# Third batch's routing and the first expert's tokens in a hash-attention and mixture-of-experts kernel: one-hot, low keys and first gathers earlier in GpSimd's row, both turns ahead of their reading, and ScalarE rounding two pieces of w2

## The chip, the cores and the metric

The kernel runs on one core of one Trainium2 chip. A core has TensorE (PE in the rows; PEld is its weight load), VectorE (DVE), ScalarE (ACT), GpSimd (POOL) and the queue of SyncE (SP) from which most transfers are issued. The metric is the time of one execution in microseconds (us), lower is better. Unprofiled executions are given as a median; a profiled one gives the rows.

## The reference

```
# attention: q, k, v of (batch 4, heads 8, seq 768, dim 64), proj (64, 6)
q_bucket, k_bucket = hash of the signs of q @ proj and k @ proj      # 6 bits
scores = where(q_bucket == k_bucket, q @ k.T / 8, -1e9)
x = (softmax(scores) @ v), heads side by side -> (3072 tokens, 512)
# experts: 8, each 512 -> 1024 -> 512
logits = x @ w_gate;  e = argmax(logits);  gate = max of softmax(logits)
eom = sigmoid(x @ w_output_gate)[e]
out[token] = gate * eom * (relu(x[token] @ w1[e]) @ w2[e])
```

Everything is float32. A product that needs float32 precision is made of three matmuls of rounded operands: each operand is split in a rounded high part and a low part (value minus high part), and high x high, high x low and low x high are added.

## The kernel before

**Attention.** 32 heads are taken as 16 pairs (8 heads per batch, so four pairs per batch), 12 steps per pair, 192 steps in all. A step is one block of 128 queries of one head against 768 keys: `scores` (8 matmuls, L609, into a buffer of `ps_s`), a minimum on VectorE (L612), `soft` (exponential on ScalarE, L620), `normal` (row sums on VectorE, L627 and L628, then one multiplication per step on GpSimd, L630), `transposed` (12 transposes, L659, and copies to `pts` by ScalarE and VectorE, L666), and, per six steps, `weighted` (24 matmuls with v, L677). `transposed` runs six steps behind `scores`. The next pair's keys and queries are split into high and low parts ahead of their use: the low keys `kl` of a head are written by GpSimd (`split_lo`, L561) and read by the third term of `scores`.

**Order.** The order on each engine is written by hand: an instruction stands in its engine's row where the program issues it, and each engine works its row in order. The main loop goes through the steps two at a time. `plan(step, f)` puts a piece of other work at the end of a step; `block(step, when, f)` puts it into a step that is a multiple of six, where the order is: scores, two exponentials, "early", normals, "amid", two exponentials, normals, "before", "matmuls" (the 24 of `weighted`), "behind", then an exponential and `transposed` of two steps.

**Routing.** When a batch's attention is done, its tokens are routed during the next batch's steps: `best` (row maximum and exponentials), `equal`, `lowest`, `one_hot`, `prefix` (matmuls that count tokens per expert), `offsets`, `own_ranks`, chunk places, columns of a table (`column2`, `column0`, `column1` on GpSimd, `hot0` to `hot2` on VectorE), `table` (6 matmuls, L266) and `entries` (VectorE adds them, L270 and L271). `ROUTE` holds the steps for this; its second row is for the third batch, whose routing begins at step 144 (18 stands for step 162).

**First expert ahead.** After the third batch the expert with the most tokens so far is picked, and 256 of its tokens start early. `early_load` (SyncE) brings w1 in four pieces, `early_w1` splits each in two halves on GpSimd (high part L1008, low part L1009, 512 of 1024 columns each), `early_gather` makes the token numbers from the table (`lead_slots` on VectorE) and issues two indirect gathers of 128 rows each on GpSimd (L295), and `early_turn` transposes them on TensorE (L309) and rounds and splits them on VectorE (L311, L312). `late` is step 168, so `late + 24` is step 192, the first one without `scores`.

**Tail.** After step 197 come, interleaved: the first expert's upward products (`fill(0)` to `fill(7)`, 12 matmuls each, L355; ScalarE's relu, L365; the low part on VectorE, `low()`, L366), `weighted` of the last block, four pieces of w2 (`w2_piece`: load, high part, low part), and the last batch's routing on VectorE, up to its table. `w2_piece(..., "h")` makes the high part on GpSimd (L180) and the low part on VectorE (L183); "hl" makes both on GpSimd, "l" the low part on GpSimd and the high part on ScalarE (L182), which no piece of the first expert has in the kernel before. Pieces 4 and 6 are loaded into the space of a `pts` buffer, pieces 0 and 2 into the two `w_raw` buffers that held w1's third and fourth pieces. After this the downward products and the other experts follow.

Of the kernel before, what the change touches and what calls it, by code (L numbers as in the profile page):

```python
# [54 lines left out]
def f32(ap):  # L55
    return ap.bitcast(F32)
# [3 lines left out]
def lsh_attention_then_moe(  # L60
# [241 lines left out]
    def turn(xgn, xs, c0, px=None):  # L302

        xg, n = xgn
        early = px is not None
        if not early:
            px = ps_t.tile([P, NCC, CH], F32, name="ps_t")
        for cc in range(NCC):
            nc.tensor.transpose(px[:, cc, 0:n], xg[0:n].rearrange("n (p b) -> n b p", b=NCC)[:, cc], ident[0:n, 0:n])  # L309
        xh, xlo = (x[:, :, c0:c0 + n] for x in xs)  # L310
        (nc.vector.tensor_copy if early else nc.scalar.copy)(xh, px[:, :, 0:n])  # L311
        nc.vector.tensor_tensor(xlo, px[:, :, 0:n], f32(xh), ALU.subtract)  # L312
# [120 lines left out]
    with ExitStack() as actx:  # L433
# [19 lines left out]
                 ((18, "best"), (20, "equal"), (22, "lowest"), (22, "one_hot"), (24, "own_ranks"), (26, "chunk_hot"),  # L453
                  (28, "chunk_pos"), (28, "gate_sums"), (30, "hot0"), (31, "column2"), (32, "gate_values"),
                  (33, "column0"), (34, "hot1"), (36, "gate_parts"), (37, "gate_product"), (37, "column1"),
# [441 lines left out]
        for b in range(B - 1):  # L897
            r = routing(b)
            s0 = 12 * (H // 2) * (b + 1)
            for hf in range(2):  # L900
                block(s0 + PER * (hf + 1), "before", lambda r=r, hf=hf: r["logits"](hf, H // 2))
            for n, when, name in ((12, "before", "tokens0"), (18, "before", "tokens1"),
                                  (30 if b < B - 2 else 24, "before", "prefix"),
                                  (30 if b < B - 2 else 24, "before", "offsets"),
                                  (48 if b < B - 2 else 42, "before", "table"),
                                  (48 if b < B - 2 else 42, "before", "entries")):
                block(s0 + n, when, r[name])
            for n, name in ROUTE[b == B - 2]:
                plan(s0 + n, r[name])
# [83 lines left out]
        def early_turn(a):  # L993
            if a == 0:
                early["x"] = new_x0()
                early["px"] = ps_s.tile([P, 2, 512], F32, name="ps_s")
            turn(early["xg"][a], early["x"], a * CH, early["px"][:, a].rearrange("p (b n) -> p b n", b=NCC))

        def early_load(cc):
            early.setdefault("raw", []).append(w1_load(0, cc))  # L1000

        def early_w1(cc, h):
            if h == 0:
                early.setdefault("w1", []).append(
                    [wpool.tile([P, F], F32R, name="w1" + n, bufs=NCC) for n in "hl"])
# [7 lines left out]
        plan(late + 18, early_gather)  # L1013
        for a in range(EARLY):
            block(late + 24, ("early", "amid")[a], lambda a=a: early_turn(a))
        for cc in range(NCC):
            plan(late + (4, 5, 11, 15)[cc], lambda cc=cc: early_load(cc))
            for h in range(2):
                if (cc, h) == (NCC - 1, 1):
                    block(late + 24, "behind", lambda cc=cc, h=h: early_w1(cc, h))  # L1020
                else:
                    plan(late + (8, 10, 13, 14, 16, 19, 20)[2 * cc + h], lambda cc=cc, h=h: early_w1(cc, h))

        with tc.manual_schedule(engines=MANUAL | {mybir.EngineType.SP}):
# [98 lines left out]
            for f in (0, 4, 6, 2):  # L1123
                raw = spare[:, (f - 4) * DM:(f - 2) * DM].rearrange("p (f d) -> p f d", f=2) if f >= 4 else None
                pieces[f] = w2_piece(ep, 0, f, "h" if f in (0, 4) else "hl", raw)
# [11 lines left out]
            fill(2)  # L1137
            r["best"]()
            low()
# [240 lines left out]
```

## Time and profile before

| | us |
|---|---|
| median of 3 runs (lowest, highest) | 705.07 (704.32, 706.34) |
| the profiled execution's own time | 706.62 |
| its span, first to last instruction | 704.8 |
| granted TensorE clock, mean over the span | 0.993 |

The span is what the rows cover; times in rows count from its start. A timeline row gives start, duration, engine, line, operation, output and inputs, the number of merged instructions, and in brackets how long the engine had been idle and what ended that. The granted clock is a share of 2.4 GHz: 1.00 is the full clock, 0.50 is 1.2 GHz.

### The profile page before, as it was taken

The page shows a single profiled execution, that of the slowest core. Times are in us where ns is not written, and L with a number is a line of the kernel's source. Part 1 is how long each engine was busy: PE and PEld are TensorE (multiplying, and loading weights), DVE is VectorE, ACT ScalarE, POOL GpSimd, SP SyncE. Part 2 cuts the span into 40 slices and gives each one's busy share as a digit, 9 for nine tenths or more (in the row PEclk, how much of TensorE's full clock was granted, in tenths as well). Part 3 has the DMA queues.
Part 4 walks back from the last instruction along what each step waited for, and adds up shares of the span by engine and source line. Part 5 has one row for each costly group of instructions (what it writes and reads, how often), then busy time and mean ns, then how long its engine had stood idle before and what let it go on. Part 6 is the DMA issues. An engine that isn't in the chain of part 4 may idle for free. (4 is left out here: it accounts for less than half of the span.)

```text
span 704.8 us, 17360 instructions
## 1 busy us (share of the span) xinstructions
PE 686.8 (97%) x6591; PEld 540.6 (77%) x6591; DVE 460.1 (65%) x1012; ACT 437.9 (62%) x894; POOL 422.5 (60%) x550
## 2 busy tenths in 40 slices
PE   8999999999999999998997999999999999999996
PEld 5667676666767676766664789889999999989895
DVE  7888887888887888876865744453536454556340
ACT  5888998889898988887975124433426253434231
POOL 6767866577765778565898646354372727374201
PEclk9999999999999999999999999999999999999999
DMA  5554544354544545433335235533455544545401
GB/s 173 148 130 105 125 120 104 86 121 119 118 106 87 128 109 120 119 69 78 109 84 138 59 95 194 204 113 118 166 166 168 158 159 161 170 142 191 155 6 43
DMA packets 85283, 87.47 MB, mean 124 GB/s; under 512 B 57167, under 2 KB 67591, under 8 KB 85192
## 3 DMA queue, kind: packets, MB, share of 16 engines
q1 hardware_dynamic: 79704, 72.88, 38.6%
q0 software_dynamic: 5200, 13.31, 5.9%
q8 instruction: 54, 0.88, 0.5%
q14 instruction: 37, 0.30, 0.1%
q10 hardware_dynamic: 288, 0.10, 0.1%
HBM read 59.57 MB, written 13.11 MB: 103 GB/s over the span
## 5 line engine op out<-in xcount | busy, mean ns | idle before, releaser
L630 POOL TENSOR_SCALAR sc<-sc,rsum 128x768 f32<-128x768 f32 x192 | 172.2, 915 | 82.1 <-ACT pts L666 41.6
L612 DVE TENSOR_SCALAR_CACHE_REDUCE sc<-ps_s 128x768 f32<-128x768 f32 x192 | 176.3, 955 | 22.6 <-PE ps_s L609 20.7
L620 ACT ACTIVATE sc<-sc,mn 128x768 f32<-128x768 f32 x192 | 178.8, 950 | 3.8 <-DVE sc L612 3.7
L609 PE MATMUL ps_s<-kh,qhl 64*128 64x384 f32 x768 | 148.2, 400 | 1.4 <-DVE sc L612 0.8
L677 PE MATMUL ps_a<-pts,vt 128*64 128x384 f32 x768 | 134.3, 500 | 0.0
L666 ACT COPY pts<-ps_t 128x384 f32<-128x384 f32 x188 | 92.8, 494 | 36.3 <-PE ps_s L659 28.7
L677 PEld LDWEIGHTS ps_a<-pts,vt 128*64 128x64 f32 x768 | 53.5, 139 | 68.6 <-issue 61.5
L366 DVE SCALAR_TENSOR_TENSOR hl<-ps_s,hh 128x256 fp32r<-128x256 f32 (+8 forms) x40 | 34.0, 849 | 108.2 <-ACT hh L365 108.2
L377 POOL DMA_INDIRECT out_dram<-yo,sid x29 | 30.8, 1063 | 112.7 <-ACT yo L372 52.0
L355 PE MATMUL ps_s<-xh,w1h 128*128 128x256 f32 (+7 forms) x288 | 96.9, 337 | 0.6 <-DVE eq L748 0.6
L659 PEld LDWEIGHTS ps_t<-ident,sc 64*128 64x128 f32 x1140 | 81.9, 139 | 20.1 <-POOL sc L630 10.2
L329 POOL DMA_INDIRECT xq<-x_dram,idx x75 | 82.6, 1101 | 23.8 <-issue 19.9
L355 PE MATMUL ps_s<-xlo,w1h 128*128 128x256 f32 (+7 forms) x288 | 95.4, 331 | 0.0
L355 PE MATMUL ps_s<-xh,w1l 128*128 128x256 f32 (+7 forms) x288 | 95.4, 331 | 0.0
L365 ACT ACTIVATE hh<-ps_s 128x256 fp32r<-128x256 f32 (+8 forms) x40 | 29.1, 727 | 96.6 <-PE ps_s L355 95.3
L659 PE MATMUL ps_t<-ident,sc 64*128 64x64 f32 x1140 | 86.5, 223 | 0.0
L609 PEld LDWEIGHTS ps_s<-kh,qhl 64*128 64x128 f32 x768 | 76.1, 187 | 4.3 <-DVE sc L612 2.2
L609 PE MATMUL ps_s<-kl,qhl 64*128 64x384 f32 x384 | 66.6, 333 | 1.4 <-POOL kl L561 1.4
L609 PE MATMUL ps_s<-bb 64*128 64x384 bf16 x384 | 65.2, 327 | 0.0
L355 PEld LDWEIGHTS ps_s<-xh,w1h 128*128 128x128 f32 x288 | 54.2, 188 | 2.5 <-PE ps_s L355 0.8
L355 PEld LDWEIGHTS ps_s<-xlo,w1h 128*128 128x128 f32 x288 | 54.2, 188 | 1.4 <-DVE xlo L312 0.2
L666 ACT COPY pts<-ps_m 128x384 f32<-128x384 f32 x94 | 45.2, 480 | 15.9 <-PE ps_m L659 14.1
(252 smaller groups left out, 1389.9 us busy)
## 6 DMA issues: line engine op xcount, KB each, us to landing
w_raw<-in_w_dram SPq DMA_DIRECT2D x34, 512.0 KB
qk<-in_qkT_dram SPq DMA_DIRECT2D x32, 384.0 KB
qhl<-qhl SPq DMA_DIRECT2D x62, 192.0 KB
xh<-in_w_dram SPq DMA_DIRECT2D x14, 512.0 KB
xlo<-in_w_dram SPq DMA_DIRECT2D x14, 512.0 KB
vt<-in_v_dram SPq DMA_DIRECT2D x16, 384.0 KB
x_dram<-xb SPq DMA_DIRECT2D x60, 96.0 KB
xq<-x_dram,idx POOLq DMA_INDIRECT x75, 3.5
```

Of the source, the lines that this page charges most:

```text
L329: nc.gpsimd.indirect_dma_start(out=xq[:, k * P:(k + 1) * P], out_offset=None, in_=x_dram.rearrange("n (a f) -> (n a) f", a=NB32), in_offse ...
L355: nc.tensor.matmul(ps, l, r, start=first and k == 0, stop=last and k == len(pairs) - 1)
L365: nc.scalar.activation(hh, ph, AF.Relu)
L366: return lambda: nc.vector.scalar_tensor_tensor(hl, ph, 0.0, f32(hh), ALU.max, ALU.subtract)
L377: nc.gpsimd.indirect_dma_start(out=out[:, :], out_offset=bass.IndirectOffsetOnAxis(ap=sid[0:n, r, a:a + 1], axis=0), in_=yo[0:n], in_offse ...
L609: nc.tensor.matmul(ss[:, h, 0:HS], q[rs, c:c + P], k[rs, 0:HS], start=(i == 0), stop=(i == 3))
L612: nc.vector.tensor_scalar(sc, ss[:, :, 0:HS], MASKED, None, ALU.min, ALU.min, accum_out=mn)
L620: nc.scalar.activation(pr, pr, AF.Exp, bias=mn, scale=-1.0, accum_out=sums[s // GROUP][:, k, 0:1])
L630: nc.gpsimd.tensor_scalar(live[s0 + k], live[s0 + k], rs[:, k:k + 1], 0.0, ALU.mult, ALU.add)
L659: nc.tensor.transpose(trs[h][:, c], pr[r, c * P:(c + 1) * P], ident[r, r])
L666: (nc.vector.tensor_copy if h and s and (last or s % PER == 0) else nc.scalar.copy)(pts[:, :, t * P + h * hq:t * P + (h + 1) * hq], trs[h])
L677: nc.tensor.matmul(st["av"][j * D:(j + 1) * D], st["v"][:, j, c], blocks[hb][j][:, c], start=(c == 0), stop=(c == NT - 1))
```

## The change

In the second row of `ROUTE`, `lowest` and `one_hot` go from step 166 to 164, and so ahead of the low keys `kl` of step 165; `column2` goes from 175 to 177, `gate_values` from 176 to 177, `column0` from 177 to 178. The first half of w1's first piece goes from 176 to 177, so that the low keys of step 177 stand ahead of all of these. For the third batch `table` and `entries` go from "before" to "early" at step 186, and `early_gather` from the end of step 186 to "early" there, ahead of the normals of that step. The first half of w1's third piece goes from 184 to 186, its second half from 187 to "behind" at 192, beside the second half of the fourth. `early_turn(0)` issues both turns' transposes ahead of any reading of them. w2's pieces are taken in the order 4, 6, 0, 2; 4 and 6 have their high parts on GpSimd and their low parts on VectorE, 0 and 2 their high parts on ScalarE and their low parts on GpSimd. One `low()` of the tail goes ahead of `best`.

```diff
--- before.py
+++ after.py
@@ -299,16 +299,19 @@
     def new_x0():
         return [gp.tile([P, NCC, CAP0], F32R, name=n) for n in ("xh0", "xlo0")]
 
-    def turn(xgn, xs, c0, px=None):
+    def turned_to(px, xgn):
 
         xg, n = xgn
-        early = px is not None
-        if not early:
-            px = ps_t.tile([P, NCC, CH], F32, name="ps_t")
         for cc in range(NCC):
             nc.tensor.transpose(px[:, cc, 0:n], xg[0:n].rearrange("n (p b) -> n b p", b=NCC)[:, cc], ident[0:n, 0:n])
+        return n
+
+    def turn(xgn, xs, c0):
+
+        px = ps_t.tile([P, NCC, CH], F32, name="ps_t")
+        n = turned_to(px, xgn)
         xh, xlo = (x[:, :, c0:c0 + n] for x in xs)
-        (nc.vector.tensor_copy if early else nc.scalar.copy)(xh, px[:, :, 0:n])
+        nc.scalar.copy(xh, px[:, :, 0:n])
         nc.vector.tensor_tensor(xlo, px[:, :, 0:n], f32(xh), ALU.subtract)
 
     def slot_rows(tacc):
@@ -450,9 +453,9 @@
                   (34, "gate_sums"), (38, "chunk_pos"), (38, "gate_values"), (39, "column2"), (40, "hot0"),
                   (42, "gate_parts"), (44, "gate_product"), (44, "hot1"),
                   (45, "column0"), (45, "column1"), (46, "hot2")),
-                 ((18, "best"), (20, "equal"), (22, "lowest"), (22, "one_hot"), (24, "own_ranks"), (26, "chunk_hot"),
-                  (28, "chunk_pos"), (28, "gate_sums"), (30, "hot0"), (31, "column2"), (32, "gate_values"),
-                  (33, "column0"), (34, "hot1"), (36, "gate_parts"), (37, "gate_product"), (37, "column1"),
+                 ((18, "best"), (20, "equal"), (20, "lowest"), (20, "one_hot"), (24, "own_ranks"), (26, "chunk_hot"),
+                  (28, "chunk_pos"), (28, "gate_sums"), (30, "hot0"), (33, "column2"), (33, "gate_values"),
+                  (34, "column0"), (34, "hot1"), (36, "gate_parts"), (37, "gate_product"), (37, "column1"),
                   (38, "hot2")))
 
         def plan(step, *fns):
@@ -902,8 +905,8 @@
             for n, when, name in ((12, "before", "tokens0"), (18, "before", "tokens1"),
                                   (30 if b < B - 2 else 24, "before", "prefix"),
                                   (30 if b < B - 2 else 24, "before", "offsets"),
-                                  (48 if b < B - 2 else 42, "before", "table"),
-                                  (48 if b < B - 2 else 42, "before", "entries")):
+                                  (48 if b < B - 2 else 42, "before" if b < B - 2 else "early", "table"),
+                                  (48 if b < B - 2 else 42, "before" if b < B - 2 else "early", "entries")):
                 block(s0 + n, when, r[name])
             for n, name in ROUTE[b == B - 2]:
                 plan(s0 + n, r[name])
@@ -993,16 +996,19 @@
         def early_turn(a):
             if a == 0:
                 early["x"] = new_x0()
-                early["px"] = ps_s.tile([P, 2, 512], F32, name="ps_s")
-            turn(early["xg"][a], early["x"], a * CH, early["px"][:, a].rearrange("p (b n) -> p b n", b=NCC))
+                px = ps_s.tile([P, 2, 512], F32, name="ps_s")
+                early["px"] = [px[:, i].rearrange("p (b n) -> p b n", b=NCC) for i in range(EARLY)]
+                for i in range(EARLY):
+                    turned_to(early["px"][i], early["xg"][i])
+            xh, xlo = (x[:, :, a * CH:(a + 1) * CH] for x in early["x"])
+            nc.vector.tensor_copy(xh, early["px"][a])
+            nc.vector.tensor_tensor(xlo, early["px"][a], f32(xh), ALU.subtract)
 
         def early_load(cc):
             early.setdefault("raw", []).append(w1_load(0, cc))
+            early.setdefault("w1", []).append([wpool.tile([P, F], F32R, name="w1" + n, bufs=NCC) for n in "hl"])
 
         def early_w1(cc, h):
-            if h == 0:
-                early.setdefault("w1", []).append(
-                    [wpool.tile([P, F], F32R, name="w1" + n, bufs=NCC) for n in "hl"])
             c = slice(h * F // 2, (h + 1) * F // 2)
             hi, lo, raw = (x[:, c] for x in (*early["w1"][cc], early["raw"][cc]))
             nc.gpsimd.tensor_scalar(hi, raw, 1.0, 0.0, ALU.mult, ALU.add)
@@ -1010,16 +1016,16 @@
 
         plan(late + 2, compare, pick)
         plan(late + 4, chosen)
-        plan(late + 18, early_gather)
+        block(late + 18, "early", early_gather)
         for a in range(EARLY):
             block(late + 24, ("early", "amid")[a], lambda a=a: early_turn(a))
         for cc in range(NCC):
             plan(late + (4, 5, 11, 15)[cc], lambda cc=cc: early_load(cc))
             for h in range(2):
-                if (cc, h) == (NCC - 1, 1):
+                if cc >= NCC // 2 and h:
                     block(late + 24, "behind", lambda cc=cc, h=h: early_w1(cc, h))
                 else:
-                    plan(late + (8, 10, 13, 14, 16, 19, 20)[2 * cc + h], lambda cc=cc, h=h: early_w1(cc, h))
+                    plan(late + (9, 10, 13, 14, 18, 0, 20)[2 * cc + h], lambda cc=cc, h=h: early_w1(cc, h))
 
         with tc.manual_schedule(engines=MANUAL | {mybir.EngineType.SP}):
             t = signs()
@@ -1120,9 +1126,9 @@
             fill(0)
             spare = tp.tile([P, NT, HS], F32, name="pts0").rearrange("p a b -> p (a b)")
             pieces = {}
-            for f in (0, 4, 6, 2):
+            for f in (4, 6, 0, 2):
                 raw = spare[:, (f - 4) * DM:(f - 2) * DM].rearrange("p (f d) -> p f d", f=2) if f >= 4 else None
-                pieces[f] = w2_piece(ep, 0, f, "h" if f in (0, 4) else "hl", raw)
+                pieces[f] = w2_piece(ep, 0, f, "h" if f >= 4 else "l", raw)
             for f in range(0, NFB, 2):
                 w2s += pieces[f]
             for c in range(NT):
@@ -1135,8 +1141,8 @@
             low()
             r["add_pair"](1, lp)
             fill(2)
+            low()
             r["best"]()
-            low()
             r["choose"]()
             rows(NP - 1, 1, False)
             fill(3)
```

## Rows read from the trace of the kernel before

**Rows 1.** The page's second part: busy tenths in 40 slices of the span.
```profile
PE   8999999999999999998997999999999999999996
```

**Rows 2.** Windows: length; busy PE, PEld, DVE, ACT, POOL; clock; DMA share; GB/s.
```profile
328.00:330.00 2.00, 2.00 (x10) 0.77 (x8) 0.00 (x0) 0.00 (x0) 2.00 (x4) 0.54 0.31 56
...
341.67:384.30 42.63, 37.99 (x471) 25.10 (x469) 28.52 (x78) 30.69 (x72) 41.12 (x51) 0.96 0.42 105
```

**Rows 3.** Timeline of TensorE: its waits, three blocks of weighted, the start of fill(0).
```profile
325.37 0.18 PE L794 MATMUL ps_m<-ohb,tri 128*128 128x48 bf16 x1 [2.34 <-POOL ohb L759]
...
325.64 5.79 PE L677 MATMUL ps_a<-pts,vt 128*64 128x384 f32 x24
...
349.67 0.44 PE L609 MATMUL ps_s<-kl,qhl 64*128 64x384 f32 x2 [1.37 <-POOL kl L561]
...
350.22 4.09 PE L677 MATMUL ps_a<-pts,vt 128*64 128x384 f32 x24
...
375.02 0.72 PE L309 MATMUL ps_s<-ident,xg 128*128 128x128 f32 x4 [1.54 <-DMA xg<-x_dram,gid]
377.25 0.94 PE L309 MATMUL ps_s<-ident,xg 128*128 128x128 f32 x4 [1.51 <-DVE rsum L627]
378.12 5.52 PE L677 MATMUL ps_a<-pts,vt 128*64 128x384 f32 x24
...
386.81 0.36 PE L355 MATMUL ps_s<-xh,w1h 128*128 128x256 f32 x1
...
397.74 0.36 PE L355 MATMUL ps_s<-xh,w1h 128*128 128x256 f32 x1 [0.61 <-DVE eq L748]
```

**Rows 4.** Timeline of GpSimd around the third batch's one-hot.
```profile
318.70 1.02 POOL L561 TENSOR_TENSOR kl<-qk,kh 128x384 fp32r<-128x384 f32 x1
322.58 1.79 POOL L630 TENSOR_SCALAR sc<-sc,rsum 128x768 f32<-128x768 f32 x2 [2.86 <-ACT pts L666]
324.34 0.27 POOL L205 TENSOR_TENSOR oneh<-ei,expi 128x48 f32<-128x48 f32 x1
...
325.29 0.51 POOL L552 TENSOR_SCALAR qhl<-qk 128x384 fp32r<-128x384 f32 x1
```

**Rows 5.** Timelines of VectorE and TensorE in the same stretch.
```profile
319.81 0.08 DVE L612 DVE_READ_ACCUMULATOR sc<-ps_s 128x1 f32 x1
...
322.30 0.18 DVE L753 TENSOR_REDUCE ei<-eq 128x6 f32<-128x48 f32 x1
...
322.50 0.35 PE L609 MATMUL ps_s<-kl,qhl 64*128 64x384 f32 x2
```

**Rows 6.** Timeline of GpSimd from the low keys to the gathers and after.
```profile
345.38 0.51 POOL L239 TENSOR_TENSOR t_rhs<-oneh,t_oa 128x192 fp32r<-128x192 f32 x1
...
366.82 3.58 POOL L630 TENSOR_SCALAR sc<-sc,rsum 128x768 f32<-128x768 f32 x4
370.59 1.21 POOL L295 DMA_INDIRECT xg<-x_dram,gid  x1 [0.19 <-DVE sc L612]
372.10 0.96 POOL L295 DMA_INDIRECT xg<-x_dram,gid  x1 [0.30 <-issue]
...
377.02 5.33 POOL L630 TENSOR_SCALAR sc<-sc,rsum 128x768 f32<-128x768 f32 x6
```

**Rows 7.** Timeline of TensorE: the first transpose of step 182.
```profile
368.65 0.21 PE L659 MATMUL ps_t<-ident,sc 64*128 64x64 f32 x1
```

**Rows 8.** Timelines of GpSimd, VectorE and ScalarE in the tail.
```profile
387.39 3.03 POOL L180 TENSOR_SCALAR w2h<-pts 128x1024 fp32r<-128x1024 f32 x2 [2.07 <-DMA pts<-in_w_dram]
...
389.44 2.05 DVE L183 TENSOR_TENSOR w2l<-pts,w2h 128x1024 fp32r<-128x1024 f32 x1 [0.94 <-POOL w2h L180]
...
393.47 0.56 DVE L680 COPY ot<-ps_a 128x384 f32<-128x384 f32 x1 [1.41 <-PE ps_a L677]
...
395.08 0.38 ACT L365 ACTIVATE hh<-ps_s 128x256 fp32r<-128x256 f32 x1 [6.19 <-PE ps_s L355]
```

**Rows 9.** Groups by line and form, whole span: ScalarE's rounding of a piece.
```profile
L182 ACT CAST w2h<-w_raw 128x1024 fp32r<-128x1024 f32 x14 | 13.9, 1045 | 0.0
```

## The prediction, made before the result was known

> **What bounds the kernel now.** I read the page's slices first, then windows of the stretch where TensorE's slices dip, then TensorE's timeline at every place where it waits, then the row of the engine that each wait names.
>
> Each slice is 17.6 us. After the first, TensorE's stay full to the last but for two, 317 to 335 us and 370 to 388 us [rows 1]; the reader is to see these dips. In and near them lie five waits [rows 3]: 2.34 us for the third batch's one-hot, 1.37 us for low keys, 1.54 us for the first gather, 1.51 us for VectorE's reading of the first turn, 0.61 us for a `ps_s` buffer. A row can name VectorE's row sum (L627) at 377.25 although the wait is for the low part ahead of it, which ends just before; I read it as L312, since the second turn writes the tile that L312 reads. After the first wait, and after the third and fourth together, the clock is halved for a while: the 24 matmuls of `weighted` take 5.79 and 5.52 us there and 4.09 us elsewhere [rows 3], and the granted clock is 0.54 from 328 to 330 us, near the lower of its two levels [rows 2]. The 1.37 us wait left the clock up: the block right behind it took 4.09 us. So TensorE sets the time, and what it has to wait for in this stretch is GpSimd's row: GpSimd is busy 41.12 of 42.63 us from 341.67 to 384.30 [rows 2]. In that stretch an edit that only reorders GpSimd's work shifts a wait unless it moves work behind all that TensorE needs. That is the question for each part.
>
> All times below are on the clock of the profile before; where TensorE has gained something, I say by how much its own times move.
>
> **Part 1, one-hot ahead of the low keys of step 165.** Nothing is added. GpSimd is idle for 2.86 us between these keys and the next normals, and the one-hot stands behind those [rows 4]. In the new place `lowest` follows VectorE's reduction that ends at 319.89: 319.89 + 0.18 = 320.07 [rows 5]. The one-hot and its cast take 0.95 us (324.34 to 325.29 [rows 4]): 320.15 to 321.1. The low keys then take 1.02 us [rows 4] and end at 322.1 to 322.2, against 319.72 before; behind them stand the normals at 322.58, which don't move. TensorE reads these keys at 322.50 [rows 5], so the move has about 0.3 us to spare. The prefix matmuls (wait till 325.37) then start as soon as the scores end, about 323.0. Gain: 2.34 us of waiting and 5.79 - 4.09 = 1.70 us of clock, **4.04 us**. `weighted` then ends near 327.3; the transposes behind it need normals that ended at 324.37 [rows 4], so nothing else is late. Bounds: 0 if the wait only changes its name, 4.04.
>
> **Part 2, low keys of step 177 first, table columns and a half of w1 behind them.** The four normals ahead end when `column2` starts, 345.38 [rows 6]; the keys then end near 346.4, two us before TensorE wants them at 349.67 - 1.37 = 348.30 [rows 3]. Gain: 1.37 us. What was moved behind (two pieces of the table and a half of w1) still stands ahead of the normals of steps 176 to 179, so these end when they did.
>
> **Part 3, table, entries and gathers in "early" at step 186.** For TensorE the table stays where it was, right behind the scores. On GpSimd the two gathers now stand ahead of the normals of steps 182 to 185, and a half of w1 that stood there goes behind them. That half takes (377.02 - 373.06) / 2 = 1.98 us, the gathers 1.21 + 0.30 + 0.96 = 2.47 us [rows 6]. So the gathers start at 366.82 - 1.98 = 364.84 and the four normals at 367.3 instead of 366.82. Each takes 3.58 / 4 = 0.895 us: step 182 is ready at 368.2, step 183 at 369.1. TensorE transposed step 182 at 368.65 [rows 7] and is now 1.37 us earlier, 367.28. It waits 0.9 us, works 0.45 us on step 182, and waits some 0.45 us for step 183: 1.35 us, which is what part 2 gained. The clock should hold, as it did at 1.37 us. I take parts 2 and 3 at **0 us** together on TensorE, bounds -0.5 (if GpSimd is another half us late) and +1.37.
>
> What they do buy is the gathers: issued 5.7 us earlier, and as 370.59 to 375.02 was 4.4 us to landing [rows 3, 6], both land by 371, ahead of TensorE's turns at 375.02 - 1.54 = 373.48.
>
> **Part 4, both turns ahead of their reading.** With the rows landed and no VectorE read between the turns, the waits of 1.54 and 1.51 us go, the second turn takes 0.72 instead of 0.94 us, and `weighted` 4.09 instead of 5.52 us [rows 3]: 3.05 + 0.22 + 1.43 = **4.70 us**. VectorE reads after both turns, which nothing on TensorE needs before the tail. Two halves of w1 (columns 512 to 1023) go behind the last normals; they still end near 384.2 (GpSimd has the same work), while `fill(0)`, which reads columns 0 to 127, comes at 386.81 - 4.7 = 382.1 [rows 3]. No row of before can show whether it waits for the other half, which was done by 384.3 [rows 2], ahead of `fill(0)`. I take no wait, since the halves are separate regions; the other end is 384.3 - 382.1 = 2.2 us and a halved clock (1.70), 3.9 us. `fill(4)`, which does need these halves, is three fills and twelve matmuls of `weighted` twice later.
>
> **Part 5, w2's pieces and the tail.** One `low()` ahead of `best` frees the buffer for `fill(3)` before VectorE's row maximum: 0.61 us gained [rows 3]. Against it: VectorE's two low parts now wait for GpSimd, which gets to w2 only after w1's halves at 384.2. The loads need 387.39 - 383.64 = 3.75 us from the end of `weighted` [rows 3, 8] and so land by 382.4, no hindrance. Two high parts in 3.03 us [rows 8], the second perhaps behind VectorE's first low part: done by 387.2. VectorE's second low part then ends at 388.4 to 389.3 (1.2 to 2.05 us [rows 8]), before it was 391.49, and behind it stand a transpose, an addition and the copy of `ot` that `add_pair` reads. That copy of 0.56 us, begun at 393.47 before [rows 8], now ends at 389.8 to 390.7; TensorE wants it after a `fill`, when it is ready for the next relu, 395.08 - 4.7 = 390.4 [rows 8]. Loss 0 to 0.4 us, taken as 0.2. ScalarE's two roundings cost 1.045 us each [rows 9] in a stretch where it idles 6.19 us [rows 8]; the second load can start at 384.2, is there at 388.0 and rounded at 389.0, and the relu that stands behind it is wanted at 395.08 - 4.7 = 390.4: free, with 1.4 us to spare. Part 5: **0.41 us**, bounds 0.2 and 0.61.
>
> From 406 us on TensorE's slices are full [rows 1], so the gains go through to the end.
>
> **Sum.** 4.04 + 0 + 4.70 + 0.41 = 9.15 us. The profiled execution takes 706.62 us, its span 704.8 plus 1.8 around it; it would come to 697.5. It lies 1.55 us above the median of 705.07, and I apply the same 9.15 us to the median: **695.9 us**.
>
> **A rule against it.** In their old place the gathers took 1.21 and 0.96 us with VectorE's reductions beside them [rows 6]. The Trainium skill, "SBUF — State Buffer", section "SBUF: two separate sides", says that a copy on VectorE can lock GpSimd out of the port with which it writes the descriptors of its own transfers. As a mechanism of this kernel: in the new place VectorE has two copies of 0.56 us nearby [rows 8]; if the gathers stand still for both, the normals come 1.1 us later and TensorE waits 1.1 us more at step 182: 8.05 us gained, 697.0 us. The old rows speak neither for nor against it, since no such copy runs beside them.
>
> **The rivals.**
> - GpSimd keeps up (its normals of 182 are there in time) and part 2's 1.37 us stays: 694.5 us. For it: in the new order the four normals end only half a us later than in the old one. Against: 96% busy. 10%.
> - The gathers stretched by copies, as above: 697.0 us. 6%.
> - One large part does not do what it says. Either the low keys of step 165 become the wait that the one-hot was (spare 0.3 us only; `lowest` behind VectorE's next reduction would use that up), or `fill(0)` waits for all of w1: at worst 4.0 us are lost, 699.9 us. For the first speaks the small margin, against it that `lowest` stands ahead of that reduction. 10%.
> - Both of these at full price: 4.04 + 3.9 us lost, 703.8 us, which is within 0.3% of before. 4%.
> - Slower: ScalarE is held in its row by the second rounding. Its load waits for the last half of w1 on GpSimd; relu, `low()` and the `ps_s` buffers stand behind it, and TensorE with them. With a halved clock behind it (1.70) it decides from a landing 3.75 + 1.4 + 9.15 + 2.1 - 1.7 = 14.7 us after issue, where 3.75 us were measured; at 18 us the loss is 18 - 5.15 + 1.7 = 14.6 us, the time 710.5 us. 4%.
> - The forecast: 66%.
>
> 0.3% is about what a measurement of this kernel tells from no change (2.1 us here). Faster by more than that: 66 + 10 + 6 + 10 = 92%; the same 4%; slower 4%. The range goes from 693.7 us (all waits gone and part 5 at its best, 9.15 + 1.37 + 0.2, and 0.6 for small terms that I left out) to 700.0 us (one large part lost).
>
> **What the profile after would show.** Part 1 is right if the prefix matmuls follow the scores without a wait, the low keys of step 165 end before TensorE's third score term of step 169, and the next `weighted` takes 4.09 us. Part 2: no wait for low keys. Part 3: the gathers stand ahead of four normals, and a wait of about 1 us shows at the transposes of steps 182 and 183. Part 4: eight transposes of the turns in one run, `weighted` after them at 4.09 us, a clock of 1.00 throughout. Part 5: no wait at `fill(3)`, at most some tenths at `add_pair`. The prediction is wrong if `fill(0)` waits for GpSimd, if a clock of 0.50 remains, or if a new wait stands at the scores of step 169.

## The result and the profile after

The changed kernel takes 696.7 us (median of 4 runs, 696.53 to 698.47) where the kernel before takes 704.86 us beside it (4 runs, 704.32 to 706.34): ratio 0.9887, 95% interval 0.9865 to 0.9909, faster by 6.4 to 9.5 us. Its profiled execution takes 696.61 us, span 694.9, mean granted clock 0.998. Line numbers are those of the changed kernel: L612 for L609, L633 for L630, L662 for L659, L680 for L677, L797 for L794, L358 for L355, all three further down, and L306 for the turns' L309; L180, L183 and L295 keep theirs.

The page's slices of the span (TensorE, its clock), and two windows (length; busy PE, PEld, DVE, ACT, POOL; clock; DMA share; GB/s):

```profile
PE   8999999999999999999999999999999999999996
...
PEclk9999999999999999999999999999999999999999
...
326.00:328.00 2.00, 2.00 (x36) 1.22 (x34) 1.42 (x6) 1.60 (x5) 2.00 (x3) 1.00 0.98 143
341.67:374.85 33.18, 31.69 (x393) 20.78 (x393) 24.54 (x69) 26.66 (x63) 31.83 (x41) 1.00 0.38 89
```

Both dips of [rows 1] are gone. The clock, 0.54 behind the first wait in [rows 2], is 1.00 there. From 341.67 to 374.85 us (the stretch of [rows 2], its end 9.45 us earlier) GpSimd is as full as before, 31.83 of 33.18 us (96%), but TensorE is now busy 31.69 us of it, also 96%, where it was busy 37.99 of 42.63 us (89%). TensorE's timeline at the places of [rows 3]:

```profile
322.71 0.20 PE L797 MATMUL ps_m<-ohb,tri 128*128 128x48 bf16 x1
...
322.99 4.09 PE L680 MATMUL ps_a<-pts,vt 128*64 128x384 f32 x24
...
364.15 0.27 PE L662 MATMUL ps_t<-ident,sc 64*128 64x64 f32 x1 [0.84 <-POOL sc L633]
...
365.03 0.27 PE L662 MATMUL ps_t<-ident,sc 64*128 64x64 f32 x1 [0.29 <-POOL sc L633]
...
369.02 1.15 PE L306 MATMUL ps_s<-ident,xg 128*128 128x128 f32 x8
370.10 4.09 PE L680 MATMUL ps_a<-pts,vt 128*64 128x384 f32 x24
...
377.36 0.36 PE L358 MATMUL ps_s<-xh,w1h 128*128 128x256 f32 x1
...
389.95 0.20 PE L797 MATMUL ps_m<-ohb,tri 128*128 128x48 bf16 x1 [0.84 <-DVE ohb L762]
...
390.74 0.39 PE L358 MATMUL ps_s<-xh,w1h 128*128 128x256 f32 x1 [0.44 <-DVE hl L369]
...
396.59 0.78 PE L266 MATMUL ps_t<-t_rhs,lt 128*128 128x128 f32 x6
```

The five waits of [rows 3] are gone. Four shorter ones have come: 0.84 and 0.29 us at the transposes of steps 182 and 183, 0.84 us at the last batch's prefix, 0.44 us at `fill(4)`; a fifth, of 0.15 us, stands at transposes that wait for GpSimd's normals at 351.22. `fill(0)` comes 386.81 - 377.36 = 9.45 us earlier than before [rows 3]. The last batch's table in the kernel before, on TensorE's timeline (the view ends ahead of its sixth matmul):

```profile
405.35 0.67 PE L266 MATMUL ps_t<-t_rhs,lt 128*128 128x128 f32 x5
```

From `fill(0)` to this table the tail took 405.35 - 386.81 = 18.54 us; it now takes 396.59 - 377.36 = 19.23. It has grown by 0.69 us.

GpSimd's timeline at the places of [rows 4, 6]:

```profile
319.87 0.27 POOL L205 TENSOR_TENSOR oneh<-ei,expi 128x48 f32<-128x48 f32 x1 [1.36 <-DVE ei L756]
...
320.81 1.01 POOL L564 TENSOR_TENSOR kl<-qk,kh 128x384 fp32r<-128x384 f32 x1
322.28 1.79 POOL L633 TENSOR_SCALAR sc<-sc,rsum 128x768 f32<-128x768 f32 x2 [0.46 <-ACT pts L669]
...
360.66 1.21 POOL L295 DMA_INDIRECT xg<-x_dram,gid  x1 [0.19 <-issue]
362.18 0.96 POOL L295 DMA_INDIRECT xg<-x_dram,gid  x1 [0.30 <-issue]
363.18 3.55 POOL L633 TENSOR_SCALAR sc<-sc,rsum 128x768 f32<-128x768 f32 x4
...
379.80 2.05 POOL L180 TENSOR_SCALAR w2h<-pts 128x1024 fp32r<-128x1024 f32 x2
383.19 5.46 POOL L183 TENSOR_TENSOR w2l<-w_raw,w2h 128x1024 fp32r<-128x1024 f32 x2 [1.34 <-ACT w2h L182]
```

and VectorE's in the tail, where [rows 8] showed the kernel before:

```profile
380.88 3.18 DVE L183 TENSOR_TENSOR w2l<-pts,w2h 128x1024 fp32r<-128x1024 f32 x2 [2.96 <-POOL w2h L180]
...
386.34 0.42 DVE L369 SCALAR_TENSOR_TENSOR hl<-ps_s,hh 128x256 fp32r<-128x256 f32 x1
386.67 0.20 DVE L741 TENSOR_REDUCE mx<-lgt 128x6 f32<-128x48 f32 x1
386.90 1.82 DVE L743 TENSOR_TENSOR df<-lgt,mx 128x48 f32<-128x48 f32 x1
388.75 0.19 DVE L751 TENSOR_SCALAR eq<-df 128x48 f32<-128x48 f32 x1
```

The reader is to see `df`: a subtraction on 128x48 that takes 1.82 us; the compare of the same size right behind it takes 0.19. It ends at 388.72, and GpSimd's second low part at 383.19 + 5.46 = 388.65. The one-hot that the prefix waits for stands behind `df`, and behind that the low part that frees the buffer of `fill(4)`. The kernel before has a shorter case of the same; its timelines of GpSimd and VectorE:

```profile
394.82 2.38 POOL L183 TENSOR_TENSOR w2l<-w_raw,w2h 128x1024 fp32r<-128x1024 f32 x1
...
396.14 1.12 DVE L740 TENSOR_TENSOR df<-lgt,mx 128x48 f32<-128x48 f32 x1
```

There `df` takes 1.12 us and ends at 397.26, GpSimd's low part at 397.20.

### The profile page after: what moved, and what is told of

It is laid out like the page before. It is cut to its first block, busy times and chain, and to the rows that moved or that the text cites. A ratio compares the mean times of both kernels' runs of the same rounds, so it can differ in the third digit from the quotient of the medians.

```text
span 694.9 us, 17362 instructions
## 1 busy us (share of the span) xinstructions
PE 683.1 (98%) x6591; PEld 539.3 (78%) x6591; DVE 460.9 (66%) x1012; ACT 440.0 (63%) x896; POOL 417.9 (60%) x548
## 5 line engine op out<-in xcount | busy, mean ns | idle before, releaser
L633 POOL TENSOR_SCALAR sc<-sc,rsum 128x768 f32<-128x768 f32 x192 | 171.9, 911 | 79.9 <-ACT pts L669 40.2
L612 PE MATMUL ps_s<-kh,qhl 64*128 64x384 f32 x768 | 148.2, 400 | 1.4 <-DVE sc L615 0.8
L680 PE MATMUL ps_a<-pts,vt 128*64 128x384 f32 x768 | 131.2, 490 | 0.0
L680 PEld LDWEIGHTS ps_a<-pts,vt 128*64 128x64 f32 x768 | 52.5, 137 | 66.3 <-issue 60.9
L662 PEld LDWEIGHTS ps_t<-ident,sc 64*128 64x128 f32 x1140 | 81.9, 139 | 22.1 <-POOL sc L633 13.2
L358 PE MATMUL ps_s<-xh,w1h 128*128 128x256 f32 (+7 forms) x288 | 96.8, 336 | 0.4 <-DVE hl L369 0.4
L358 PE MATMUL ps_s<-xlo,w1h 128*128 128x256 f32 (+7 forms) x288 | 95.4, 331 | 0.0
L358 PE MATMUL ps_s<-xh,w1l 128*128 128x256 f32 (+7 forms) x288 | 95.3, 331 | 0.0
L662 PE MATMUL ps_t<-ident,sc 64*128 64x64 f32 x1140 | 86.9, 223 | 1.3 <-POOL sc L633 1.3
L612 PEld LDWEIGHTS ps_s<-kh,qhl 64*128 64x128 f32 x768 | 76.2, 187 | 4.4 <-DVE sc L615 2.2
L612 PE MATMUL ps_s<-kl,qhl 64*128 64x384 f32 x384 | 66.6, 333 | 0.0
L612 PE MATMUL ps_s<-bb 64*128 64x384 bf16 x384 | 65.3, 327 | 0.0
L358 PEld LDWEIGHTS ps_s<-xh,w1h 128*128 128x128 f32 x288 | 54.2, 188 | 2.3 <-issue 0.6
L358 PEld LDWEIGHTS ps_s<-xlo,w1h 128*128 128x128 f32 x288 | 54.2, 188 | 1.4 <-DVE xlo L315 0.2
```

Source lines behind the costliest of these rows:

```text
L358: nc.tensor.matmul(ps, l, r, start=first and k == 0, stop=last and k == len(pairs) - 1)
L612: nc.tensor.matmul(ss[:, h, 0:HS], q[rs, c:c + P], k[rs, 0:HS], start=(i == 0), stop=(i == 3))
L633: nc.gpsimd.tensor_scalar(live[s0 + k], live[s0 + k], rs[:, k:k + 1], 0.0, ALU.mult, ALU.add)
L662: nc.tensor.transpose(trs[h][:, c], pr[r, c * P:(c + 1) * P], ident[r, r])
L680: nc.tensor.matmul(st["av"][j * D:(j + 1) * D], st["v"][:, j, c], blocks[hb][j][:, c], start=(c == 0), stop=(c == NT - 1))
```

## The experiments

Each run stands beside runs of the kernel before on the same chip; with ratios (the changed kernel's is 0.9887) their medians can be compared. The intervals reach 1 to 1.6 us to each side, so the times do not tell two variants apart that differ by less than about 2 us: there the profile's waits decide.

**Part 1 undone** in the changed kernel:

```diff
-(20, "lowest"), (20, "one_hot")
+(22, "lowest"), (22, "one_hot")
```

> The changed kernel with part 1 alone undone (lowest and one_hot back at step 166). My theory: the wait of about 2.3 us for the one-hot and a halved clock come back, 4.0 to 4.3 us more than the changed kernel, about 4.5 us under the kernel before. Rival: the other parts gave TensorE slack there, and less than 2 us come back.

701.27 us against 705.34, ratio 0.9944 (0.9923 to 0.9965). TensorE's timeline:

```profile
325.00 0.18 PE L797 MATMUL ps_m<-ohb,tri 128*128 128x48 bf16 x1 [2.34 <-POOL ohb L762]
...
325.27 5.79 PE L680 MATMUL ps_a<-pts,vt 128*64 128x384 f32 x24
```

The wait and the slow `weighted` are back exactly as in [rows 3], and all later waits are those of the changed kernel (0.85, 0.30, 0.88, 0.44 us). Part 1 is worth 2.34 + 1.70 us, and the ratios differ by 4.0 us.

**Part 1 alone** in the kernel before:

```diff
-(22, "lowest"), (22, "one_hot")
+(20, "lowest"), (20, "one_hot")
```

> The kernel before with part 1 alone (lowest and one_hot at step 164). My theory: the 2.34 us wait for the one-hot and the halved clock behind it go, weighted takes 4.09 us there, 4.0 to 4.3 us less, ratio about 0.994; the other four waits stay. Rival: the low keys of step 165, now behind the one-hot, become the wait at the scores of step 169, and the time falls by under 1 us.

702.66 us against 705.34, ratio 0.9954 (0.9937 to 0.9971): 3.2 us less (2.0 to 4.4), where 4.0 to 4.3 were expected. The wait is gone, those of parts 2 to 5 stay (1.25, 1.19, 1.51, 0.59 us). From the block of `weighted` ahead of part 1 to the one behind it TensorE takes 337.17 - 315.62 = 21.55 us, before 337.95 - 312.33 = 25.62: 4.07 us gained in its place. The profiled execution, at 706.10 us the slowest of the six, has a span of 704.4 us all the same, only 0.4 less than before. It lost 3.4 us at the start, ahead of all that was changed: its first block of `weighted` starts at 29.77 us, before at 26.37. And the 24 matmuls of `weighted` behind the turns took 6.36 us, 0.84 more than before, with a low clock; windows around them:

```profile
375.00:379.00 4.00, 3.00 (x10) 1.50 (x12) 2.75 (x8) 1.46 (x4) 4.00 (x5) 0.50 0.86 192
379.00:383.00 4.00, 4.00 (x20) 1.55 (x16) 0.00 (x0) 0.00 (x0) 3.92 (x5) 0.67 0.00 0
```

Why this execution started late is not known.

**Part 2 undone** in the changed kernel:

```diff
-(33, "column2"), (33, "gate_values"), (34, "column0")
+(31, "column2"), (32, "gate_values"), (33, "column0")
-plan(late + (9, 10, 13, 14, 18, 0, 20)[...
+plan(late + (8, 10, 13, 14, 18, 0, 20)[...
```

> The changed kernel with part 2 undone (table columns and the half of w1 ahead of the low keys of step 177 again). My theory: the wait for the low keys comes back (1.0 to 1.4 us) and the waits at the transposes of steps 182 and 183 (0.84 and 0.30 us) shrink by about as much, so that fill(0) starts within 0.4 us of where it does in the changed kernel. Rival: GpSimd is not the bound there, the waits at 182 and 183 stay, and the time is 1.0 to 1.4 us longer.

697.73 us against 705.34, ratio 0.989 (0.9872 to 0.9908). TensorE's timeline:

```profile
345.74 0.44 PE L612 MATMUL ps_s<-kl,qhl 64*128 64x384 f32 x2 [1.26 <-POOL kl L564]
```

The wait for low keys is back, and those of steps 182 and 183 shrink from 1.13 to 0.28 us. TensorE's work ends at 690.27 us, with part 2 at 689.68; but 0.43 of these 0.59 us were there ahead of part 2's place (the block of `weighted` at 312.55 for 312.12). Of 1.26 us, under 0.2 stay. That GpSimd's row gives back most of a gain upstream is shown.

**Part 3 undone** in the changed kernel (table and entries in "before", the gathers at the end of step 186):

```diff
-"before" if b < B - 2 else "early", "table"
+"before", "table"        (and the same for "entries")
-block(late + 18, "early", early_gather)
+plan(late + 18, early_gather)
```

> The changed kernel with part 3 undone: table and entries in before, gathers at the end of step 186, behind all four normals, the halves of w1 as in the changed kernel. My theory: no wait at steps 182 and 183 (1.14 us gained), but the second gather lands about 2 us after TensorE could start the turns, so a wait of 1.5 to 2 us stands there: 0.3 to 1 us longer than the changed kernel, the clock stays up. Rival: gathers ahead of the normals were needed in full, the wait at the turns is 3 us or more with a halved clock behind it, 3 us longer.

698.14 us against 704.36, ratio 0.9912 (0.9895 to 0.9929). No wait is left at steps 182 and 183; at the turns TensorE waits instead:

```profile
368.66 1.60 PE L306 MATMUL ps_s<-ident,xg 128*128 128x128 f32 x8 [0.75 <-DMA xg<-x_dram,gid]
```

From there to the start of `weighted` at 370.19 are 1.53 us, 0.45 more than in the changed kernel, since the second turn waits for its rows too (0.3 us at its weight load). TensorE ends at 689.56 us, as in the changed kernel. In the profile, moving the gathers ahead of the normals exchanges waits of 1.20 us for waits of 1.13. By the ratios this run is 1.8 us behind the changed kernel, but the intervals overlap: whether part 3 gains anything is open.

**Table and gathers in "amid"**, between the two:

```diff
-"early", "table"  /  "early", "entries"  /  block(late + 18, "early", early_gather)
+"amid", "table"   /  "amid", "entries"   /  block(late + 18, "amid", early_gather)
```

> The changed kernel with table, entries and gathers of step 186 in amid, between the normals of steps 182 and 183 and those of 184 and 185. My theory (GpSimd's row is what step 182 waits for): the waits of 0.84 and 0.30 us at steps 182 and 183 go, a wait of 0.3 to 0.6 us appears at steps 184 and 185, which now stand behind the gathers; the gathers still land ahead of the turns; 0.5 to 0.8 us less than the changed kernel. Rival: the whole of it moves to steps 184 and 185, no change.

699.1 us against 704.36, ratio 0.9926 (0.9911 to 0.994): a miss, 2.7 us behind the changed kernel by the ratios. The waits of 0.84 and 0.29 us shrink to 0.38 and 0.29 at steps 184 and 185, but a new one of 2.39 us stands in the tail. Timelines of TensorE, VectorE and GpSimd:

```profile
387.96 0.85 PE L735 MATMUL ps_m<-wgt,ot 128*128 128x32 f32 x6 [2.39 <-DVE ot L683]
...
381.48 5.38 DVE L183 TENSOR_TENSOR w2l<-pts,w2h 128x1024 fp32r<-128x1024 f32 x2 [3.58 <-POOL w2h L180]
...
382.99 6.09 POOL L183 TENSOR_TENSOR w2l<-w_raw,w2h 128x1024 fp32r<-128x1024 f32 x2 [0.53 <-ACT w2h L182]
```

GpSimd's high parts came 0.6 us later (380.41 for 379.80), and VectorE's low parts, which wait for them, with them. GpSimd's first low part waits for ScalarE and came at 382.99, ahead of VectorE's second (383.5; in the changed kernel 382.8 and GpSimd's 383.19). VectorE's two took 5.38 instead of 3.18 us, and behind TensorE's wait the clock was 0.50 from 390 to 393 us. `df`, which came when GpSimd's low parts were done, took 0.21 us.

**Part 4's turns alone** in the kernel before (both turns' transposes ahead of VectorE's reading, nothing else):

```diff
 def early_turn(a):
...
+        for i in range(EARLY):
+            xg, n = early["xg"][i]
+            for cc in range(NCC):
+                nc.tensor.transpose(early["px"][i][:, cc, 0:n], ...)
-    turn(early["xg"][a], early["x"], a * CH, ...)
+    nc.vector.tensor_copy(xh, early["px"][a])
+    nc.vector.tensor_tensor(xlo, early["px"][a], f32(xh), ALU.subtract)
```

> The kernel before with both turns' transposes ahead of their reading, the gathers where they were. My theory: the wait of 1.51 us for VectorE shrinks to what the second gather's landing leaves (about 0.2 us), the wait of 1.54 us for the first gather stays; if with that the clock stays up, 1.3 + 1.6 = 2.9 us less, if not, 1.3 us less. Rival: the second turn waits for something else (the second gather lands later than VectorE was done), and nothing is gained.

704.86 us against 705.34, ratio 0.9993 (0.9976 to 1.0009): no difference that the times can tell. TensorE's timeline:

```profile
374.73 0.72 PE L1001 MATMUL ps_s<-ident,xg 128*128 128x128 f32 x4 [1.11 <-DMA xg<-x_dram,gid]
376.08 0.75 PE L1001 MATMUL ps_s<-ident,xg 128*128 128x128 f32 x4 [0.64 <-DMA xg<-x_dram,gid]
376.76 4.09 PE L677 MATMUL ps_a<-pts,vt 128*64 128x384 f32 x24
```

Both turns wait for their rows, 1.75 instead of 3.05 us, and in this execution the clock holds; `fill(3)` then waits 1.43 instead of 0.61 us. The order of the turns needs the earlier gathers to show in the times. The profiled span is 3.1 us shorter than before's (1.2 of it behind the last matmul) and the median is not: why the two differ is not settled. No run put the turns back in the changed kernel, so what their order is worth there is read from its profile alone.

**Part 4's halves undone**: w1's third piece split at 184 and 187 again.

```diff
-if cc >= NCC // 2 and h:
+if (cc, h) == (NCC - 1, 1):
-plan(late + (9, 10, 13, 14, 18, 0, 20)[...
+plan(late + (9, 10, 13, 14, 16, 19, 20)[...
```

> The changed kernel with w1's third piece split where the kernel before split it: its first half at step 184, its second at 187, and only the fourth piece's second half behind the last normals. Theory (GpSimd's row sets the time here; moving the half behind is what made the early gathers and the normals of steps 182 to 185 affordable): the half of 1.98 us stands ahead of these normals again, the waits at the transposes of steps 182 and 183 grow from 0.84 + 0.30 us to about 3.1 us together, 2.0 us more; if the clock halves behind the longer wait, 1.7 to 3.4 us more on top. 698.7 us with the clock kept, up to 702 us without. Rival (the same work in another order, and the wait of 1.1 us has another cause): 696.7 us, waits as in the changed kernel.

700.46 us against 706.15, ratio 0.993 (0.991 to 0.9949). TensorE's wait, and the window behind it:

```profile
366.12 0.27 PE L662 MATMUL ps_t<-ident,sc 64*128 64x64 f32 x1 [2.81 <-POOL sc L633]
...
367.40:370.80 3.40, 3.40 (x39) 3.01 (x36) 1.47 (x3) 1.10 (x3) 3.32 (x5) 0.51 0.02 5
```

2.81 + 0.29 us, as worked out, and the clock at 0.51 behind it; 3.0 us behind the changed kernel by the ratios. Moving a half of w1 behind the last normals is what pays for the early gathers.

**w2's pieces undone**: order 0, 4, 6, 2 on the engines of before.

```diff
-for f in (4, 6, 0, 2):
+for f in (0, 4, 6, 2):
-    "h" if f >= 4 else "l"
+    "h" if f in (0, 4) else "hl"
```

> The changed kernel with w2's pieces in the order 0, 4, 6, 2 and on the engines that they had in the kernel before (pieces 0 and 4: high part on GpSimd, low part on VectorE; 6 and 2: both parts on GpSimd); the low part ahead of the row maximum stays. Theory (the new order of the pieces is needed because of part 4: piece 0's buffer is held by the halves of w1 that now end near 379.8 us, and its load, with those of 4 and 6 queued behind it, comes 3.75 us later): GpSimd starts on w2 near 383.6 instead of 379.8 us and has about 8.2 us of work, VectorE's low parts and its steps from row maximum to one-hot are held longer, and the prefix matmuls wait 1 to 3 us longer than the 0.85 us of the changed kernel: 697.7 to 699.7 us. Rival (the new share is itself what costs the 0.7 us that the tail is longer than forecast): without it the tail is as short as before, 695.4 to 696.0 us.

703.12 us against 706.15, ratio 0.9957 (0.9941 to 0.9972), 4.9 us behind the changed kernel by the ratios, 2 us more than the most that was expected. Timelines of TensorE, VectorE and GpSimd:

```profile
388.08 1.49 PE L735 MATMUL ps_m<-wgt,ot 128*128 128x32 f32 x6 [2.55 <-DVE ot L683]
...
391.42 2.42 DVE L751 TENSOR_SCALAR eq<-df 128x48 f32<-128x48 f32 x1
...
391.41 2.39 POOL L183 TENSOR_TENSOR w2l<-w_raw,w2h 128x1024 fp32r<-128x1024 f32 x1
```

Piece 0 now waits for w1's halves, all pieces come later, and TensorE waits 2.55 us for VectorE at `add_pair`, with a halved clock behind it (0.50 from 388 to 392 us; the matmuls took 0.41 instead of 0.28 us). The compare `eq` is held beside GpSimd's last low part here; `df` ahead of it took 1.10 us beside GpSimd's last high part (390.29 to 391.33). Part 5's pieces bring no gain over the kernel before; they save what part 4 would have cost without them.

**The low part undone**: `best` ahead of it again.

```diff
-            low()
             r["best"]()
+            low()
```

> The changed kernel with one low part of the tail back behind the row maximum and its subtraction. Theory (GpSimd's last low part holds VectorE's subtraction for some 1.8 us): the low part waits behind the held subtraction, fill(3) waits 1.3 to 1.5 us for its buffer, the prefix then follows fill(3) without its wait of 0.85 us, so the loss is 0.3 to 0.7 us: 697.0 to 697.4 us, with a wait of over 1 us at fill(3) in the profile. Rival (the term as the prediction had it: 0.61 us at fill(3), nothing else changes): 697.3 us, with a wait of 0.6 us at fill(3) and that of 0.85 us at the prefix still there. The profile's waits tell these apart, not the time.

698.49 us against 706.15, ratio 0.9901 (0.9881 to 0.992). TensorE's timeline:

```profile
389.00 0.36 PE L358 MATMUL ps_s<-xh,w1h 128*128 128x256 f32 x1 [1.49 <-DVE eq L751]
```

`fill(3)` waits 1.49 us and the prefix and `fill(4)` no more: the theory's wait, not the 0.61 us of the prediction's term. `fill(4)` starts at 390.74 as in the changed kernel: where the low part stands matters little as long as `df` is held. By the ratios the run is 1.0 us behind, expected 0.3 to 0.7.

**`mx` in PSUM**, so that `df` reads one operand in SBUF and one in PSUM:

```diff
-mx = gp.tile([P, NT], F32, name="mx")
+mx = ps_t.tile([P, NT], F32, name="ps_t") if b == B - 1 else gp.tile(...)
```

> The changed kernel with the last batch's row maximum mx kept in PSUM, so that the subtraction df on VectorE (L743, 1.82 us in the changed kernel, 0.23 us for the third batch) reads one operand from SBUF and one from PSUM. My theory: df was held by GpSimd's low part of w2's last piece, through the SBUF port the two share; with one operand in PSUM it takes 0.2 to 0.3 us beside the same GpSimd instruction, the wait of 0.85 us for the one-hot ahead of prefix goes, that of 0.44 us at fill(4) too: 0.8 to 1.3 us less. Rival: df waits for its input or is long by itself in this place, and stays at 1 us or more.

697.37 us against 704.36, ratio 0.9904 (0.9886 to 0.9922). VectorE's timeline:

```profile
386.85 0.20 DVE L743 TENSOR_TENSOR df<-lgt,ps_t 128x48 f32<-128x48 f32 x1
387.09 1.57 DVE L751 TENSOR_SCALAR eq<-df 128x48 f32<-128x48 f32 x1
```

`df` is free, and the next instruction is held in its place, until 388.66, while GpSimd's low part ends at 383.15 + 5.46 = 388.61. The prefix waits 0.60 instead of 0.84 us, and the time doesn't move, where 0.8 to 1.3 us less were expected.

**GpSimd's low parts in halves**, 128x512 each (VectorE's stay whole):

```diff
-nc.gpsimd.tensor_tensor(lo, raw, f32(hi), ALU.subtract)
+for j in range(2):
+    nc.gpsimd.tensor_tensor(lo[:, j], raw[:, j], f32(hi[:, j]), ALU.subtract)
```

> The changed kernel with GpSimd's low parts of w2's two pieces each as two instructions of half the size (128 x 512, about 1.27 us, in place of 2.7 us). My theory: df on VectorE waits for one GpSimd instruction that is under way, so for 1.3 us at most; it falls from 1.82 us to between 0.3 and 1.5 us and the wait ahead of prefix by as much. Rival: the time of df follows GpSimd's whole work there, not one instruction, and stays at 1.8 us or grows.

697.81 us against 704.36, ratio 0.9911 (0.9894 to 0.9927). VectorE's timeline:

```profile
387.13 0.85 DVE L747 TENSOR_TENSOR df<-lgt,mx 128x48 f32<-128x48 f32 x1
388.01 1.20 DVE L755 TENSOR_SCALAR eq<-df 128x48 f32<-128x48 f32 x1
```

GpSimd's last two halves ran from 386.63 to 387.90 and from 387.88 to 389.16. The first held `df`, the second `eq`, each to its end; the prefix waits 0.87 us, in the changed kernel 0.84: no gain.

**GpSimd's last low part behind the search** for the lowest index (`later` holds it back; the copy of `ei` makes GpSimd wait for VectorE):

```diff
             def choose():
                 ...
                 one_hot()
+                nc.gpsimd.tensor_copy(gp.tile([P, NT], F32, name="seen"), st["ei"])
+                later.pop()()
```

> The changed kernel with GpSimd's last low part (piece 2 of w2) behind the reduction that ends the lowest-index search: GpSimd first copies that reduction's 128x6 result to a scratch tile, which makes it wait, and then does the low part. Theory (this low part holds VectorE's subtraction or compare through the port that both need): the subtraction takes 0.2 instead of 1.82 us, the one-hot is ready near 388 us, the prefix and fill(4) follow without their waits of 0.85 and 0.44 us, 1.3 us gained: 695.4 us. The low part then ends near 390.5 us, and the downward products that need it come later than 395 us. Rival (the subtraction waits for its operands or for TensorE's result, not for the port): waits and time as in the changed kernel, 696.7 us. A second rival: the hold moves on to the gates' steps on VectorE and to the table, whose chain ends no earlier: the two waits go, and as much comes back at the table's matmuls, 696.7 us.

701.53 us against 706.15, ratio 0.9929 (0.9912 to 0.9946): 3.0 us behind the changed kernel by the ratios, where 1.3 us ahead was expected. Timelines of VectorE, GpSimd and TensorE (here L748 is `df`, L767 `ohb`, L186 the low part, L804 the prefix):

```profile
387.69 0.21 DVE L748 TENSOR_TENSOR df<-lgt,mx 128x48 f32<-128x48 f32 x1
...
388.88 2.38 DVE L767 CAST ohb<-oneh 128x48 bf16<-128x48 f32 x1
...
388.86 2.35 POOL L186 TENSOR_TENSOR w2l<-w_raw,w2h 128x1024 fp32r<-128x1024 f32 x1
...
391.32 0.20 PE L804 MATMUL ps_m<-ohb,tri 128*128 128x48 bf16 x1 [1.43 <-DVE ohb L767]
```

With GpSimd out of the way all steps from `df` to the one-hot took 0.2 us each: the cause is shown. But the low part was released one instruction too early. It began 0.02 us ahead of the cast `ohb` and held it for its whole length; the prefix waited 1.43 us, and the clock was 0.50 behind it, from 393.2 to 396.4 us. The copy would have had to read `ohb`, not `ei`. That version was not run; the 1.3 us that it might give are an estimate, from the waits of 0.84 and 0.44 us.

## Why the prediction was right, and which term was not

The time came out within the range and within 1 us of the forecast, in the main by the forecast mechanism: every wait of [rows 3] went and the clock stayed up. By its own terms, on TensorE:

- **Part 1**, forecast 4.04 us: the transposes behind `weighted` come 331.35 - 327.01 = 4.34 us earlier. Of this 0.21 us belong to no part: the profile after is ahead by as much at the block of `weighted` in front of part 1 (312.12 for 312.33). So part 1 gave 4.13 us. The low keys end at 321.82, 0.4 us ahead of their reading. Undoing it costs 4.0 us by the ratios (0.9944 - 0.9887).
- **Parts 2 and 3**, forecast 0 (1.37 gained, 1.35 given back at steps 182 and 183): 1.13 us given back there and 0.15 at 351.22. At the turns TensorE is 375.02 - 1.54 - 369.02 = 4.46 us ahead, so 0.12 us is left. The gathers start at 360.66 + 4.34 = 365.0 on the clock of before, forecast 364.84. They took 1.21 and 0.96 us as before, although VectorE's two copies of 0.56 us (which read PSUM) ran beside the first of them and behind it, from 361.07 to 362.17: the rival of the stretched gathers did not come. That the early gathers buy the turns is only half shown: with the gathers behind the normals and the half of w1 out of their way (part 3 undone) the turns lose 0.75 + 0.45 us and the normals nothing.
- **Part 4**, forecast 4.70 us: no wait at the turns, 4.09 us for `weighted`, and the turns take 1.08 us from start to start of what follows, where 0.72 + 0.72 were reckoned. 9.45 - 4.46 = 4.99 us, 0.3 more than forecast. `fill(0)` did not wait for w1's last half, which ended at 379.83, 2.5 us behind its start: the halves are separate for the reader too.
- **Part 5**, forecast +0.41 us, bounds 0.2 and 0.61, measured 18.54 - 19.23 = -0.69: the step that failed. Its single steps came true: no wait at `fill(3)` (0.61 gained), the copy of `ot` in time for `add_pair` (it ends at 385.11 + 4.34 = 389.45, forecast 389.8 to 390.7), and ScalarE's two roundings (1.05 us each) without delay for the relu. (By its own terms w2's loads land by 383.64 - 4.70 + 3.75 = 382.7, not 382.4; nothing hangs on it.) What was left out is that GpSimd's two low parts, 383.19 to 388.65, now lie beside VectorE's steps from row maximum to one-hot. The working asked when VectorE's low parts wait for GpSimd's results, not which VectorE instruction GpSimd holds while it works. 0.84 + 0.44 us of new waits less 0.61 gives the loss. The trace of before had the hold: its wait of 0.61 us at `fill(3)` stood behind a `df` of 1.12 us, where the third batch's took 0.23, so it was not the row maximum (0.20 us) that kept `low()` late.

0.21 + 4.13 + 0.12 + 4.99 - 0.69 = 8.76; TensorE's last matmul ends 8.75 us earlier. The two errors of the forecast, +0.5 up to `fill(0)` (9.24 without the 0.21, forecast 8.74) and -1.1 behind it, half cancel: it owes some of its closeness to that. The profiled execution gained 10.0 us, since the stretch behind the last matmul was also 1.1 us shorter in it; the medians differ by 8.2 us, forecast 9.15.

What holds VectorE is told by the changed kernel and four of the experiments (`mx` in PSUM, low parts in halves, w2's pieces undone, last low part behind). The subtraction `df` (two operands in SBUF), the compare `eq` and the cast `ohb` (both from SBUF to SBUF) are held, whichever comes while GpSimd's low part is under way, and to its end; a row maximum (0.20), a low part of `fill` with an operand in PSUM (0.42) and `df` with `mx` in PSUM (0.20) pass beside it. The Trainium skill, "SBUF — State Buffer", section "SBUF: two separate sides", says it as a rule: the port pair that VectorE and GpSimd share is an exclusive lock, taken by whichever starts first for its whole instruction, and on VectorE an instruction with two operands in SBUF (against a GpSimd instruction that reads SBUF) or in its two-port mode needs it. The rows agree, down to the 0.02 us that decided in the last experiment (GpSimd's low part at 388.86, `ohb` at 388.88); in which mode `eq` and `ohb` ran no row tells.

## What to carry to other kernels

When a bounding engine's row is only reordered, work out what is late next and by how much: here 1.28 of 1.37 us came back at the normals that followed. What lasted was a move into GpSimd's idle time (part 1) and work moved behind everything that TensorE needs (w1's half). When work is given to GpSimd, list the small VectorE instructions that will run beside it with two operands in SBUF, or as a compare or cast from SBUF to SBUF: each long GpSimd instruction can hold one of them up to its whole length (2.42 us for `eq`, alone 0.19), and what counts is whether that one is on the path. In the trace at hand, look for small instructions that take longer than elsewhere, like the `df` of 1.12 us. The clock can make a wait cost more than its length (2.34 us cost 4.04; 1.49 us at `fill(3)` with the low part undone left it at 1.00), and a part tried alone can show nothing, as the turns did. Before a profile's span is compared, see where it was lost: 3.4 us of one profile here went at the kernel's start.

## What was not expected of the hardware

Halving GpSimd's low parts did not cut the hold down: they held two VectorE instructions (0.85 and 1.20 us) instead of one (1.82). And its direction turns on small shifts: GpSimd's high parts 0.6 us later made VectorE's large low part the loser (5.38 for 3.18 us for the two), with 2.39 us of waiting on TensorE.
